# Another order of loads, weight preparation and attention at the start of a fused attention and feed-forward kernel

## The chip, the core and the metric

One core of a Trainium2 chip runs the whole program. Its engines work side by side, each through its own list of instructions in order: TensorE (PE in the profile; its weight loads are PEld), VectorE (DVE), ScalarE (ACT), GpSimd (POOL), and SyncE (SP), which here only starts DMA transfers. An engine that waits for a semaphore holds back everything behind it in its list. The metric is device microseconds from one execution; three timed runs of the kernel before gave 820.78, 822.68 and 823.08 us, so the median is 822.68 us.

## What is computed

```
kv  = einsum('bhsd,bhse->bhde', k, v)          # 8 batches, 8 heads, 576 tokens, head size 64
out = einsum('bhsd,bhde->bhse', q, kv)
x   = out / sqrt(mean(out*out, -1) + 1e-6) * g_norm     # then 4608 tokens x 512
h   = x @ w_in                                  # 512 x 2048
g   = h * tanh(softplus(h))                     # "mish"
y   = g @ w_out                                 # 2048 x 512
```

All in float32, except that the given w_in and w_out are float64, whose two 32-bit words the kernel puts together itself.

## The kernel before, in words

**Tiles and products.** The 4608 tokens are nine tiles of 512. The kernel first makes `g` for all tiles (attention and the first product), writing it to DRAM, and then the second product. Every large float32 operand is split into a high and a low part of the type fp32r (`split`, lines 129 to 131: a cast on ACT at line 130, a subtraction on DVE at line 131), and a product is three matmuls: high by high, high by low, low by high. From tile 1 on, the first product is made with seven block products instead of eight; tile 0 uses the plain eight ("whole" products, `whole_group`).

**Weight units.** `w_in` is cut into eight units (0 to 7). Each goes through six steps (`weight_in`): LOAD (four DMAs of 256 KB of raw words, SP), SCALE (ACT, line 145: the high words read as floats, multiplied), JOIN (DVE, lines 140 to 142: the low words' bits put in), BLOCKS (the split of the four blocks into the tile `wfb`), DIFF and SUMS (differences of blocks on DVE, lines 208 to 210, and their split; needed by the seven-product form). Steps of half a unit are `part_of`. Raw words lie until JOIN in a tile named either `w64` or `wfb<n>`, the place that a later unit's blocks will take. Before, unit 1 loads to the place of wfb5, 2 to wfb6, 3 to wfb7, 5 to wfb6 and 6 to wfb7, and units 0, 4 and 7 to `w64`; so the load of unit 4 waits for the join of unit 0, 5 for that of 2, 6 for that of 3 and 7 for that of 4.

**Slots.** The work is laid out by hand in numbered slots, one slot for one block product of 12 or 24 matmuls. In slot `t` first come evictions (`then`), then the product, then whatever `at(t, ...)` has put there, in the order in which the calls of `at` were made. Each engine's list keeps this order; nothing is reordered later. Tile 0 has slots 0 to 31; pairs of units are used in slots 0 to 7 (units 0, 1), 8 to 15 (2, 3), 16 to 23 (4, 5) and 24 to 31 (6, 7). In slots 24 and on, a slot uses both units of its pair. Tile 1 starts at slot 32 (`T1_`).

**Attention ahead.** While tile 0's products run, the same slots prepare the x of tile 1. `k_load` (line 269) loads a pair of heads of k and v, four pairs a batch, into tiles `km` and `vm` of three buffers each; `k_product` (line 296) multiplies two pairs; `k_keep` (lines 306, 308 on ACT, 311 on DVE) copies the result. For each half `u` of the heads: "transpose" (line 362, PE), "turned" (line 375, a copy out of PSUM on ACT), "project" (line 391, PE), "square" and "scaled" (lines 406 and 414, ACT). Later "sums" (line 430, PE), "rstd" (lines 439 to 441, ACT: a table load, Ln, Exp, and then the table for mish again), "keep" and "spread" (SP, through DRAM), "normalize" (DVE, line 459). Mish (line 127, ACT) empties the product's PSUM banks of names `a` and `bc`, two of each.

**The beginning.** Ahead of slot 0, tile 0's own x is made, with `filler` matmuls of an identity in between (line 687; one filler is two matmul instructions in the trace).

Of the kernel before, what the change touches and what calls it, by code (L numbers as in the profile page):

```python
# [34 lines left out]
def linear_attention_rms_mish_ffn(  # L35
# [622 lines left out]

    conv = {j: weight_in(j, wf_room({1: 5, 2: 6, 3: 7, 5: 6, 6: 7}[j]) if j % 4 and j < 7 else w64_room) for j in range(NF2)}
    LOAD, SCALE, JOIN, BLOCKS, DIFF, SUMS = range(6)  # L660
# [28 lines left out]
    def part_of(j, step, k):  # L689
        conv[j][step](k)  # L690
# [14 lines left out]
    weights(3, LOAD)  # L705
    for r in (slice(0, D), slice(D, P)):
        nc.gpsimd.dma_start(gcol[r, :], g_norm.rearrange("(p o) -> p o", o=1))
    make_identity(nc, ident)
# [8 lines left out]
    def do0(u, m, *steps):  # L717
        for step in steps:
            units[0][u][step](m)

    filler(8)
    do(0, 0, "transpose", "turned")
    filler(10)
    first_kv(0)
    k_keep(0, 0)
    part_of(0, SCALE, 0)
    do(0, 0, "project")
    do0(0, 0, "square")
    do0(0, 1, "square")
    filler(2)  # L730
    part_of(1, SCALE, 0)
    part_of(0, JOIN, 0)
    part_of(1, JOIN, 0)
    do0(0, 0, "sums")
    do0(0, 1, "sums")
    do0(0, 0, "rstd")
    part_of(0, BLOCKS, 0)
    do0(0, 1, "rstd")
    do(0, 1, "transpose")
    do0(0, 0, "normalize")  # L740
# [14 lines left out]
    def slot1():  # L755
        do(0, 1, "project")
        part_of(1, JOIN, 1)
        do0(1, 0, "square")
        do0(1, 1, "square")
        part_of(0, BLOCKS, 1)  # L760
        part_of(2, SCALE, 0)
        part_of(2, JOIN, 0)
        weights(4, LOAD)
        k_load(1, 0)
        k_load(1, 1)
        rows[1] = att.tile([P, H, TR, D], F32, name="qs")
        rows_load(1, 0, H)

    def slot2():
        do0(1, 0, "sums")  # L770
        do0(1, 1, "sums")
        do0(1, 0, "rstd")
        do0(1, 1, "rstd")
        do0(1, 0, "normalize")
        x_whole(A12)
# [14 lines left out]
    T1_ = start(1)  # L790
    for j, t, t2 in ((3, 5, 7), (4, 8, 10), (5, 9, 11), (6, 13, 15), (7, 16, 18)):
        if j > 3:
            at(t, lambda j=j: weights(j, SCALE))
        at(t, lambda j=j: weights(j, JOIN))
        at(t2, lambda j=j: weights(j, BLOCKS))
    for j, t in zip(range(NF2), (19, 21, 23, 25, T1_ + 6, T1_ + 8, T1_ + 13, T1_ + 15)):
        at(t, lambda j=j: weights(j, DIFF))
        at(t + 1, lambda j=j: weights(j, SUMS))
    at(1, lambda: weights(5, LOAD))
    at(1, lambda: k_load(1, 2))  # L800
    at(4, lambda: weights(6, LOAD))
# [15 lines left out]
    def attention(j):  # L817

        def spread():
# [368 lines left out]
```

## Time and profile before

| | |
|---|---|
| median of three timed runs | 822.68 us (820.78 to 823.08) |
| the profiled execution, its own time | 814.41 us |
| its span, first to last instruction | 812.4 us |
| PE busy | 792.8 us (98%) |
| DVE busy | 588.7 us (72%) |
| ACT busy | 443.0 us (55%) |
| PE idle in 0 to 40 us | 7.3 us |
| PE idle in 40 to 60 us | 4.5 us |

In the profile's rows a time is counted from the start of the span. A row of the timeline holds the start, the length, the engine, the line, the operation, the tiles written and read, the shape, how many instructions were merged, and in brackets how long the engine was idle before it and what ended that. "PEclk" is the TensorE clock granted in a stretch, as a share of full speed. The profiled execution was 8.3 us shorter than the median of the timed runs.

### The profile page before, as it was taken

To read this page: it belongs to the slowest core of one execution; us is meant where nothing else is said; L and a number is where in the kernel's file an instruction comes from. 1 tells how busy PE (TensorE), PEld (TensorE's weight loads), DVE (VectorE), ACT (ScalarE), POOL (GpSimd) and SP (SyncE) were. 2 spreads that over 40 slices of the span, in tenths; PEclk is the share of its full clock that TensorE was granted. 3 is DMA by queue.
4 is the path that set the end of the run, shared out by engine and by line. 5 is a ranking of instruction groups with operands and counts; after the bars stand their busy time and mean duration, and the time that the engine had idled before them with its cause. 6 is when DMAs were issued, how large, how long until landed. Compare 5 with 4: busy or idle time off the path is not lost.

```text
span 812.4 us, 16560 instructions
## 1 busy us (share of the span) xinstructions
PE 792.8 (98%) x6752; PEld 723.6 (89%) x6752; DVE 588.7 (72%) x777; ACT 443.0 (55%) x677; POOL 99.1 (12%) x163
## 2 busy tenths in 40 slices
PE   7879999999999999999999999999999999999997
PEld 6779899999999999899999988888888888888886
DVE  2786774668485776757566788888888888878885
ACT  4758575656565566655556654444444444444442
POOL 1011111231323222131311100000000000000000
PEclk9989999999999999999999999999999999999999
DMA  8886787778797887765478943334444444444421
GB/s 298 234 286 189 228 276 214 259 243 303 256 317 260 279 301 201 266 202 194 163 248 283 404 165 130 130 131 139 146 130 130 130 130 130 131 139 146 146 87 53
DMA packets 102859, 164.46 MB, mean 202 GB/s; under 512 B 9088, under 2 KB 69248, under 8 KB 102784
## 3 DMA queue, kind: packets, MB, share of 16 engines
q1 hardware_dynamic: 89184, 116.42, 46.4%
q0 software_dynamic: 13504, 46.93, 15.3%
q8 instruction: 53, 0.87, 0.4%
q14 instruction: 22, 0.18, 0.1%
q10 hardware_dynamic: 96, 0.07, 0.0%
HBM read 106.89 MB, written 56.49 MB: 201 GB/s over the span
## 4 chain that ended last, share of the span: by engine, by line
PE 76%; DMA 6%; issue 6%; DVE 6%; ACT 4%; SPq 2%; POOL 1%; POOLq 0%; ACTq 0%; DVEq 0%
PE a L614 17%; PE a L964 15%; PE bc L614 13%; PE bc L964 11%; PE a L969 8%; PE bc L969 6%; DMA vm<-in_v_dram 2%; DMA wfb<-wod 2%; PE x L397 1%; PE s L296 1%; DMA qs<-in_q_dram 1%; PE ss L430 1%; ACT wfb L130 1%; PE bc L687 1%; PE ss L296 1%
## 5 line engine op out<-in xcount | busy, mean ns | idle before, releaser
L130 ACT CAST gf<-g 128x1024 fp32r<-128x1024 f32 (+1 forms) x104 | 106.5, 1039 | 98.9 <-DVE g L922 64.7
L131 DVE TENSOR_TENSOR gf<-g,gf 128x1024 fp32r<-128x1024 f32 (+1 forms) x104 | 124.1, 1206 | 43.8 <-ACT gf L130 43.7
L964 PE MATMUL a<-wfb,gf 128*128 128x512 f32 x408 | 143.2, 394 | 0.3 <-ACT ow L526 0.3
L614 PE MATMUL a<-gf,wfb 128*128 128x256 f32 x960 | 129.2, 284 | 4.2 <-ACT gf L130 2.7
L614 PEld LDWEIGHTS a<-gf,wfb 128*128 128x128 f32 x960 | 120.5, 192 | 7.7 <-ACT gf L130 3.0
L969 PE MATMUL a<-wfb,gf 128*128 128x256 f32 x408 | 113.1, 277 | 0.0
L614 PE MATMUL bc<-gf,wfb 128*128 128x256 f32 x840 | 109.3, 285 | 0.4 <-DVE gf L131 0.3
L614 PEld LDWEIGHTS bc<-gf,wfb 128*128 128x128 f32 x840 | 104.1, 192 | 4.7 <-issue 2.4
L964 PE MATMUL bc<-wfb,gf 128*128 128x512 f32 x272 | 95.1, 394 | 0.0
L964 PEld LDWEIGHTS a<-wfb,gf 128*128 128x128 f32 x408 | 76.5, 188 | 18.4 <-ACT ow L526 0.6
L969 PEld LDWEIGHTS a<-wfb,gf 128*128 128x128 f32 x408 | 76.5, 188 | 0.0
L969 PE MATMUL bc<-wfb,gf 128*128 128x256 f32 x272 | 75.3, 277 | 0.0
L635 DVE TENSOR_TENSOR ula<-bc,ula 128x512 f32<-128x512 f32 x32 | 22.0, 687 | 58.4 <-PE bc L614 58.4
L964 PEld LDWEIGHTS bc<-wfb,gf 128*128 128x128 f32 x272 | 51.0, 188 | 11.9
L614 PE MATMUL bc<-gf,wfa 128*128 128x256 f32 x384 | 52.0, 285 | 1.2 <-ACT ulb L127 1.2
L127 ACT ACTIVATE ur<-ur 128x1024 f32<-128x1024 f32 x32 | 33.9, 1059 | 35.2 <-DVE ur L635 35.2
L614 PEld LDWEIGHTS a<-a,wfb 128*128 128x128 f32 x384 | 48.3, 192 | 5.0 <-DVE w L150 2.5
L614 PE MATMUL a<-a,wfb 128*128 128x256 f32 x384 | 51.9, 284 | 0.0
L614 PE MATMUL a<-gf,wfa 128*128 128x256 f32 x384 | 51.6, 284 | 0.3
L614 PEld LDWEIGHTS bc<-gf,wfa 128*128 128x128 f32 x384 | 48.3, 191 | 3.6 <-issue 1.5
L969 PEld LDWEIGHTS bc<-wfb,gf 128*128 128x128 f32 x272 | 51.0, 188 | 0.0
L614 PEld LDWEIGHTS a<-gf,wfa 128*128 128x128 f32 x384 | 48.3, 192 | 1.3 <-ACT ur L539 0.7
(205 smaller groups left out, 1433.4 us busy)
## 6 DMA issues: line engine op xcount, KB each, us to landing
g<-gd SPq DMA_DIRECT2D x18, 2048.0 KB
gd<-ur POOLq DMA_DIRECT2D x36, 512.0 KB, 4.8
gd<-ula POOLq DMA_DIRECT2D x36, 256.0 KB, 4.1
gd<-ulb POOLq DMA_DIRECT2D x36, 256.0 KB, 4.7
w<-in_moe_w_out_dram SPq DMA_DIRECT2D x32, 256.0 KB
km<-in_k_dram SPq DMA_DIRECT2D x28, 288.0 KB
vm<-in_v_dram SPq DMA_DIRECT2D x28, 288.0 KB
wfb<-in_moe_w_in_dram SPq DMA_DIRECT2D x20, 256.0 KB
```

The lines of the kernel that those rows point to most:

```text
L127: nc.scalar.activation(o, i, AF.Mish)
L130: nc.scalar.copy(hi, src)
L131: nc.vector.tensor_sub(lo, src, hi.bitcast(F32))
L296: nc.tensor.matmul(outs[a][half(o, a)], kt[half(o), d], vt[half(o), d], start=(c == 0), stop=(c == 8))
L397: nc.tensor.matmul(st["x"][a][half(o), c], kv[r], st["q"][r, a, c], start=True, stop=True)
L430: nc.tensor.matmul(to if j >= T32 else to.rearrange("p (m n) -> p m n", m=2), sel, of, start=True, stop=True)
L614: nc.tensor.matmul(bank[:, jj], w[:, a, kc, :], xf[:, b, kc, :], start=first and jj == kc == s == 0, stop=(kc == 1 and s == 2), skip_group ...
L635: nc.vector.tensor_add(o, bank, o)
L687: nc.tensor.matmul(b[:, 0:P], ident, ident, start=True, stop=True)
L964: nc.tensor.matmul(bank.rearrange("p s (h n) -> p s h n", h=2), gf[:, 0, c, :], wo_form(c, right).rearrange("p h s n -> p s h n"), start=f ...
L969: nc.tensor.matmul(bank[:, 0], gf[:, 1, c, :], wo_form(c, right)[:, :, 0, :], start=False, stop=c == NF2 - 1, skip_group_check=True)
```

## The change

The change has four parts.

1. **Places of the raw words.** Units 1, 2, 3 load to the places of wfb5, wfb6, wfb7 as before; units 4, 5, 6 to wfb4, wfb5, wfb6; only 0 and 7 to `w64`. The load of unit 4 now waits for the last read of tile 0's q (which lies in wfb4), 5 for the join of 1, 6 for that of 2, 7 for that of 0. The loads of units 4 and 5 are issued earlier, those of 6 and 7 behind batch 1's fourth k, v pair.
2. **The head of the program.** The two small DMAs of `gcol` stand behind the identity and the constants on POOL; fillers go from 8, 10, 2, 4 to 4, 7, 2, 0; unit 1's SCALE stands ahead of "square" on ACT; BLOCKS and "normalize" of the first half change places.
3. **Weight steps in the slots.** BLOCKS of unit 4 move from slot 10 to 9; units 6 and 7 from slots 13/15 and 16/18 to 18/20 and 20/22; DIFF and SUMS of units 0 and 1 from slots 19 to 22 to slots 12 to 15.
4. **Attention of tile 1 in the slots.** Batch 1's k products move from slots 7 and 13 to 10 and 17, and tile 1's steps from "transpose" (11) to "spread" (23) one slot later each.

```diff
-    conv = {j: weight_in(j, wf_room({1: 5, 2: 6, 3: 7, 5: 6, 6: 7}[j]) if j % 4 and j < 7 else w64_room) for j in range(NF2)}
+    conv = {j: weight_in(j, w64_room if j in (0, 7) else wf_room(j if j > 3 else j + 4)) for j in range(NF2)}
...
-    for r in (slice(0, D), slice(D, P)):
-        nc.gpsimd.dma_start(gcol[r, :], g_norm.rearrange("(p o) -> p o", o=1))
     make_identity(nc, ident)
...
-    filler(8)
+    for r in (slice(0, D), slice(D, P)):
+        nc.gpsimd.dma_start(gcol[r, :], g_norm.rearrange("(p o) -> p o", o=1))
+
+    filler(4)
     do(0, 0, "transpose", "turned")
-    filler(10)
+    filler(7)
     first_kv(0)
     k_keep(0, 0)
     part_of(0, SCALE, 0)
+    part_of(1, SCALE, 0)
     do(0, 0, "project")
     do0(0, 0, "square")
     do0(0, 1, "square")
     filler(2)
-    part_of(1, SCALE, 0)
     part_of(0, JOIN, 0)
     part_of(1, JOIN, 0)
     do0(0, 0, "sums")
     do0(0, 1, "sums")
-    do0(0, 0, "rstd")
     part_of(0, BLOCKS, 0)
+    do0(0, 0, "rstd", "normalize")
+    part_of(1, BLOCKS, 0)
+    x_whole(A11)
     do0(0, 1, "rstd")
-    do(0, 1, "transpose")
-    do0(0, 0, "normalize")
-    x_whole(A11)
+    do(0, 1, "transpose", "turned")
     do0(0, 1, "normalize")
-    part_of(1, BLOCKS, 0)
     x_whole(A21)
-    do(0, 1, "turned")
-    filler(4)
+    weights(4, LOAD)
...
-        weights(4, LOAD)
+        weights(5, LOAD)
         k_load(1, 0)
         k_load(1, 1)
...
+        k_load(1, 2)
...
-    for j, t, t2 in ((3, 5, 7), (4, 8, 10), (5, 9, 11), (6, 13, 15), (7, 16, 18)):
+    for j, t, t2 in ((3, 5, 7), (4, 8, 9), (5, 9, 11), (6, 18, 20), (7, 20, 22)):
...
-    for j, t in zip(range(NF2), (19, 21, 23, 25, T1_ + 6, T1_ + 8, T1_ + 13, T1_ + 15)):
+    for j, t in zip(range(NF2), (12, 14, 23, 25, T1_ + 6, T1_ + 8, T1_ + 13, T1_ + 15)):
         at(t, lambda j=j: weights(j, DIFF))
         at(t + 1, lambda j=j: weights(j, SUMS))
-    at(1, lambda: weights(5, LOAD))
-    at(1, lambda: k_load(1, 2))
-    at(4, lambda: weights(6, LOAD))
-    at(8, lambda: weights(7, LOAD))
     for n in range(2):
-        at((7, 13)[n], lambda n=n: k_product(1, n))
-        at((8, 14)[n], lambda n=n: k_keep(1, n))
-    at(7, lambda: k_load(1, 3))
+        at((10, 17)[n], lambda n=n: k_product(1, n))
+        at((11, 18)[n], lambda n=n: k_keep(1, n))
+    at(10, lambda: k_load(1, 3))
+    at(10, lambda: weights(6, LOAD))
+    at(11, lambda: weights(7, LOAD))
...
-            (0, 11, "transpose"), (0, 12, "turned"), (0, 13, "project", "square", "scaled"), (1, 15, "transpose"),
-            (1, 16, "turned"), (1, 18, "project", "square", "scaled"), (1, 20, "sums"),
-            (1, 21, "rstd"), (1, 22, "keep"), (0, 23, "spread0"), (0, 28, "normalize"), (1, 29, "normalize"),
+            (0, 12, "transpose"), (0, 13, "turned"), (0, 14, "project", "square", "scaled"), (1, 16, "transpose"),
+            (1, 17, "turned"), (1, 19, "project", "square", "scaled"), (1, 21, "sums"),
+            (1, 22, "rstd"), (1, 23, "keep"), (0, 24, "spread0"), (0, 28, "normalize"), (1, 29, "normalize"),
```

What this does to the engines' lists is shown at three places. In the rows, L145 is a SCALE, L130 into `wfb` a cast of BLOCKS or (behind `wd`) of SUMS, L140 to L142 a JOIN, L131 into `wfb` the subtraction of BLOCKS or SUMS, L306, L308 and L311 a `k_keep`, L375 "turned", L406 and L414 "square" and "scaled", and L127 a mish or the load of its table.

ACT from unit 4's SCALE (slot 8) to the first projection's "square". Before:

```order
L145 ACTIVATE wfa_616<-w_418 128x1024
L306 COPY kv_125<-s_123 128x64
L308 COPY ky_127<-ss 128x64
L145 ACTIVATE wfa_646<-wfb_434 128x1024
L130 CAST wfb_666<-wfa_616 128x4x256
L130 CAST wfb_682<-wfa_646 128x4x256
L375 COPY fh<-x_685 128x1024
L127 ACTIVATE ula<-a 128x512
L145 ACTIVATE wfa_722<-wfb_508 128x1024
L406 ACTIVATE fa<-x_764 128x1024
```

And in the changed kernel:

```order
L145 ACTIVATE wfa_558<-wfb_307 128x1024
L130 CAST wfb_577<-wfa_558 128x4x256
L145 ACTIVATE wfa_580<-wfb_411 128x1024
L130 CAST wfb_659<-wfa_580 128x4x256
L306 COPY kv_125<-s_123 128x64
L308 COPY ky_127<-ss 128x64
L127 ACTIVATE ula<-a 128x512
L130 CAST wfa_712<-wd 128x2x256
L130 CAST wfb_277<-wd 128x2x256
L375 COPY fh<-x_689 128x1024
L127 ACTIVATE ur<-a 128x2x256
L406 ACTIVATE fa<-x_737 128x1024
```

Unit 4's cast now stands ahead of unit 5's SCALE, and "turned" stands behind `k_keep`, one mish and the two casts of unit 0's SUMS.

DVE at the same place, from unit 5's JOIN. Before:

```order
L140 TENSOR_SCALAR wfa_646<-wfa_646 128x1024
L141 SCALAR_TENSOR_TENSOR wfa_646<-wfb_434,wfa_646 128x1024
L142 SCALAR_TENSOR_TENSOR wfa_646<-wfb_434,wfa_646 128x1024
L131 TENSOR_TENSOR wfb_666<-wfa_616,wfb_666 128x4x256
L131 TENSOR_TENSOR wfb_682<-wfa_646,wfb_682 128x4x256
```

And in the changed kernel, where unit 4's subtraction comes first:

```order
L131 TENSOR_TENSOR wfb_577<-wfa_558,wfb_577 128x4x256
L140 TENSOR_SCALAR wfa_580<-wfa_580 128x1024
L141 SCALAR_TENSOR_TENSOR wfa_580<-wfb_411,wfa_580 128x1024
L142 SCALAR_TENSOR_TENSOR wfa_580<-wfb_411,wfa_580 128x1024
L131 TENSOR_TENSOR wfb_659<-wfa_580,wfb_659 128x4x256
L311 COPY ky_127<-s_123 64x64 x2
L311 COPY kv_125<-ss 64x64 x2
L208 TENSOR_TENSOR wd<-wfa_247 128x512
L209 TENSOR_TENSOR wd<-wfa_247,wd 128x256
L210 TENSOR_TENSOR wd<-wfa_247,wd 128x256
L131 TENSOR_TENSOR wfa_712<-wd,wfa_712 128x2x256
L131 TENSOR_TENSOR wfb_277<-wd,wfb_277 128x2x256
```

The join of unit 5 moved behind the subtraction of unit 4, and `k_keep` and DIFF of unit 0 follow the blocks of unit 5.

ACT from the second projection's "square" on. Before, with unit 7's cast just ahead:

```order
L130 CAST wfb_880<-wfa_845 128x4x256
L406 ACTIVATE fh<-x_883 128x1024
L414 ACTIVATE gf<-x_883,gcol 128x2x2x256
L130 CAST wfa_941<-wd 128x2x256
L130 CAST wfb_286<-wd 128x2x256
L127 ACTIVATE ula<-a 128x512
L439 ACT_TABLE_LOAD
L440 ACTIVATE fl<-ss,eps 128x512
L441 ACTIVATE fl<-fl 128x512
L127 ACT_TABLE_LOAD
```

And in the changed kernel:

```order
L406 ACTIVATE fh<-x_891 128x1024
L414 ACTIVATE gf<-x_891,gcol 128x2x2x256
L130 CAST wfb_932<-wfa_867 128x4x256
L145 ACTIVATE wfa_935<-w_668 128x1024
L127 ACTIVATE ula<-a 128x512
L127 ACTIVATE ur<-a 128x2x256
L130 CAST wfb_973<-wfa_935 128x4x256
L439 ACT_TABLE_LOAD
L440 ACTIVATE fl<-ss,eps 128x512
L441 ACTIVATE fl<-fl 128x512
L127 ACT_TABLE_LOAD
L127 ACTIVATE ulb<-bc 128x512
```

Unit 6's cast, unit 7's SCALE and unit 7's cast moved behind the second projection, and the table loads and "rstd" stand behind unit 7's cast.

More of the change, by code (lines that the diff above doesn't have):

```diff
@@ L771, in slot2 @@
         do0(1, 1, "sums")
-        do0(1, 0, "rstd")
+        do0(1, 0, "rstd", "normalize")
         do0(1, 1, "rstd")
-        do0(1, 0, "normalize")
         x_whole(A12)
@@ L795, in linear_attention_rms_mish_ffn @@
         at(t2, lambda j=j: weights(j, BLOCKS))
-    for j, t in zip(range(NF2), (19, 21, 23, 25, T1_ + 6, T1_ + 8, T1_ + 13, T1_ + 15)):
+    for j, t in zip(range(NF2), (12, 14, 23, 25, T1_ + 6, T1_ + 8, T1_ + 13, T1_ + 15)):
         at(t, lambda j=j: weights(j, DIFF))
         at(t + 1, lambda j=j: weights(j, SUMS))
-    at(1, lambda: weights(5, LOAD))
-    at(1, lambda: k_load(1, 2))
-    at(4, lambda: weights(6, LOAD))
-    at(8, lambda: weights(7, LOAD))
     for n in range(2):
-        at((7, 13)[n], lambda n=n: k_product(1, n))
-        at((8, 14)[n], lambda n=n: k_keep(1, n))
-    at(7, lambda: k_load(1, 3))
+        at((10, 17)[n], lambda n=n: k_product(1, n))
[3 more added lines that the diff above has]
+    at(11, lambda: weights(7, LOAD))
     for b in range(2, B):
         t = start(b - 2)
-        loads, made = ((21, 22, 23, 28), (27, T1_ + 2)) if b == 2 else ((0, 3, 10, 11), (9, 17)) if b == 3 else (
+        loads, made = ((22, 23, 24, 28), (27, T1_ + 2)) if b == 2 else ((0, 3, 10, 11), (9, 17)) if b == 3 else (
             (18 - NS, 19 - NS, 1, 2) if b == 4 else (11 - NS, 12 - NS, 1, 2), (0, 10))
```

## The prediction, made before the change was run

> **What bounds the kernel now.** The page comes first: its span and its first row.
>
> ```profile
> span 812.4 us, 16560 instructions
> PE 792.8 (98%) x6752; PEld 723.6 (89%) x6752; DVE 588.7 (72%) x777; ACT 443.0 (55%) x677; POOL 99.1 (12%) x163
> ```
>
> PE is idle for 19.6 us in all, so only that idle time and PE time at a low clock can be won. The view of busy time by stretch shows where they lie (columns: stretch, length, busy time and instructions of PE, PEld, DVE, ACT, POOL, then PEclk, DMA share, GB/s).
>
> ```profile
> 20.30:39.88 19.58, 17.32 (x188) 14.48 (x188) 15.44 (x28) 14.51 (x25) 0.00 (x0) 1.00 0.82 234
> 39.88:51.11 11.23, 11.23 (x157) 10.89 (x156) 9.05 (x13) 6.16 (x10) 2.05 (x3) 1.00 1.07 332
> 51.11:55.58 4.47, 0.00 (x1) 0.03 (x1) 4.40 (x5) 1.62 (x2) 0.00 (x0) 0.78 1.05 372
> 55.58:60.46 4.88, 4.88 (x104) 4.23 (x105) 3.61 (x4) 2.52 (x4) 0.72 (x1) 0.50 0.37 121
> 60.46:77.86 17.40, 17.40 (x167) 15.89 (x167) 10.99 (x18) 14.01 (x20) 2.00 (x3) 1.00 0.60 186
> 93.56:280.00 186.44, 185.90 (x2140) 175.29 (x2140) 121.51 (x191) 111.95 (x187) 46.48 (x72) 1.00 0.80 262
> ```
>
> One hole of 4.47 us stands out, followed by 4.88 us at half clock, which cost another 2.44 us. But DVE was busy for 4.40 of those 4.47 us: it was not waiting. The view of waits names what PE waited for, and the timeline of ACT shows what else was late.
>
> ```profile
> PE ss L296 <- DMA vm<-in_v_dram: 4.5, 1, 4.5
> 53.96 1.04 ACT L130 CAST wfb<-wfa 128x1024 fp32r<-128x1024 f32 x1 [3.17 <-DVE wfa L142]
> 54.91 1.00 ACT L375 COPY fh<-x 128x1024 f32<-128x1024 f32 x1
> 59.80 1.03 ACT L406 ACTIVATE fa<-x 128x1024 f32<-128x1024 f32 x1 [2.36 <-PE x L391]
> ```
>
> PE's wait is for batch 1's fourth v. The copy "turned", without which the first projection can't start, began only at 54.91, behind unit 5's cast, which waited 3.17 us for a join. So two things were late at once: the DMA until 55.58, the preparation of weights until 55.91. Taking the first away leaves the second.
>
> **The change part by part.** *Loads.* With places of their own, units 4 and 5 and the fourth pair come earlier. In the trace the DMA share is 1.05 during the hole: the data were queued behind units 5 and 6, whose loads had waited on joins. In the change the pair follows the k product of slot 10 and leads unit 6, and its own product comes at slot 17, seven slots later: over 10 us for 0.6 MB at the 372 GB/s of the row above, some 2 us. That wait goes. The new waits on SP are for tile 0's q, long read by then, and for unit 1's join, whose last row is
>
> ```profile
> 28.29 0.69 DVE L142 SCALAR_TENSOR_TENSOR wfa<-wfb,wfa 128x512 uint32<-128x512 uint32 x1
> ```
>
> Behind that wait stand batch 1's loads, first needed in slot 10; it ends near 27 with the head's gain, when the queue still holds unit 4. Units 6 and 7 land later but are scaled only in slots 18 and 20.
>
> *The head.* These rows are of the timelines of POOL, PE, SP and ACT.
>
> ```profile
> 1.30 1.21 POOL L707 DMA_DIRECT2D gcol<-in_g_norm_dram  x2 [0.84 <-POOLq L1172]
> 3.13 3.78 PE L687 MATMUL bc<-ident 128*128 128x128 f32 x16 [3.13 <-POOL ident masks.py:199]
> 9.48 1.29 SPq L172 DMA_DIRECT2D w<-in_moe_w_in_dram  x2
> 11.14 0.27 PE L296 MATMUL s<-wfb,wfb 64*64 64x64 f32 x2
> 12.20 0.23 PE L296 MATMUL ss<-wfb,wfb 64*64 64x64 f32 x2
> 12.48 1.50 SPq L172 DMA_DIRECT2D wfb<-in_moe_w_in_dram  x1
> 14.42 0.60 ACT L402 ACTIVATE fa<-x 128x512 f32<-128x512 f32 x1 [1.07 <-PE x L391]
> 15.39 0.67 ACT L145 ACTIVATE wfa<-wfb 128x512 f32<-128x512 f32 x1
> 20.30 0.38 PE L614 MATMUL a<-gf,wfb 128*128 128x256 f32 x1 [1.42 <-ACT gf L130]
> ```
>
> POOL's 1.21 us leave the path to the identity, so PE starts near 1.9; fewer fillers let the first k product start when its v has landed (SP's issue at 9.48 had waited for it), at 9.5 to 9.9 instead of 11.14: 1.5 us. Then unit 1's SCALE, now ahead of the squares on ACT, waits for its words (SP's issue at 12.48 had waited for them) and ends near 13.2; the squares start there, 1.2 us early instead of 1.5. Behind them unit 1's join no longer delays "normalize", worth about another microsecond. I take the first product at 18.1: **2.2 us won**. Bounds: 1.25, if the clock stays at half through the k product (it would then take twice the 1.06 us from 11.14 to 12.20); 2.6, set by the words at 12.48. From there to slot 7 every engine's order is as before, so the gain passes through whole.
>
> *The preparation chain.* These are DVE's rows of units 3 and 5, the copies of `k_keep` and unit 0's DIFF.
>
> ```profile
> 40.15 0.69 DVE L140 TENSOR_SCALAR wfa<-wfa 128x1024 uint32<-128x1024 uint32 x1
> 42.12 1.22 DVE L142 SCALAR_TENSOR_TENSOR wfa<-wfb,wfa 128x1024 uint32<-128x1024 uint32 x1
> 44.47 1.23 DVE L131 TENSOR_TENSOR wfb<-wfa,wfb 128x1024 fp32r<-128x1024 f32 x1 [1.12 <-ACT wfb L130]
> 45.30 1.16 ACT L145 ACTIVATE wfa<-w 128x1024 f32<-128x1024 f32 x1
> 49.74 0.46 DVE L311 COPY ky<-s 64x64 f32<-64x64 f32 x2
> 52.70 1.23 DVE L142 SCALAR_TENSOR_TENSOR wfa<-wfb,wfa 128x1024 uint32<-128x1024 uint32 x1
> 71.05 0.68 DVE L208 TENSOR_TENSOR wd<-wfa 128x512 f32<-128x512 f32 x1
> 72.22 0.42 DVE L210 TENSOR_TENSOR wd<-wfa,wd 128x256 f32<-128x256 f32 x1
> ```
>
> A JOIN takes 3.2 us (40.15 to 43.34), its cast 1.05 on ACT, its subtraction 1.23, a DIFF 1.6 (71.05 to 72.64). Before, from unit 3's join to the end of unit 5's it took 13.8 us (40.15 to 53.93). In the change this stretch loses the copies (0.95), gains unit 4's subtraction (1.23) and 1.1 us in which DVE waits for unit 4's cast: 15.1 us. With the 2.2 us won, unit 3's join starts at 37.95 and unit 5's ends at 53.1. Then unit 5's cast to 54.15, its subtraction to 55.4, the copies to 56.35, DIFF to 57.95, and on ACT the two casts of SUMS, 0.6 each overlapped to 1.1, all of which now stand ahead of "turned": it starts at 59.1 and ends at **60.1**, against 55.91 before.
>
> PE meanwhile has no DMA to wait for. Before, slot 7 ended at 39.88; at 2.2 us less it is 37.7. Slots 8 to 14 at 1.44 us each, a k product of 1.2 and a transpose of 0.8 (rows below, from each start to the next) end at 49.8. So PE stands for **10 us** before the projection in slot 14. Before, the projection began at 57.4, with as much PE work behind it (one slot less, one k product more, row at 57.35): the change is 2.7 us late here. Half clock follows again: by the row of 4.88 us it costs 2.4 us after 60.1, against 1.55 that were left of it before after 57.35: 0.9 more.
>
> [...]
>
> *Units 6 and 7.* Rows of PE from slot 7's k product to the first products of tile 1, and of ACT at "rstd".
>
> ```profile
> 39.88 0.27 PE L296 MATMUL s<-vm,km 64*64 64x64 f32 x2
> 41.09 3.14 PE L614 MATMUL a<-gf,wfb 128*128 128x256 f32 x24
> 46.95 1.03 PE L362 MATMUL x<-ident,qs 128*128 128x128 f32 x8
> 57.35 0.31 PE L391 MATMUL x<-fh,kv 64*64 64x32 f32 x2
> 69.38 0.98 PE L614 MATMUL bc<-gf,wfb 128*128 128x256 f32 x6
> 72.44 0.62 PE L430 MATMUL ss<-fa,sel 128*32 128x512 f32 x2
> 74.33 1.28 ACT L439 ACT_TABLE_LOAD   x1
> 78.29 0.60 ACT L127 ACTIVATE ur<-a 128x512 f32<-128x512 f32 x1
> 90.77 1.60 PE L614 MATMUL a<-gf,wfb 128*128 128x256 f32 x12
> 93.56 1.80 PE L614 MATMUL bc<-gf,wfa 128*128 128x256 f32 x12 [1.19 <-ACT ulb L127]
> ```
>
> Let p be the end of the second projection (slot 19; before it ended at 69.4, a slot earlier in the order). From p, ACT has "square" and "scaled" to p+2.0, unit 6's cast to p+3.0, unit 7's SCALE to p+4.15; DVE its JOIN to p+7.4; then cast to p+8.5 and subtraction to p+9.75. PE reaches unit 7 in the middle of slot 24 after four slots, "sums" (1.0) and half a slot: p+7.5. It waits 1.0 us for the cast and, two matmuls later, 1.0 for the subtraction: **2.0 us**. Behind unit 7's cast come the table loads and "rstd", 3.96 us (74.33 to 78.29), and only then the mish that frees slot 26's bank, done at p+13.05, when slot 25 ended at p+11.7: **1.35 us**. The second projection itself waits some **0.5 us** for its `k_keep`, which stands behind unit 6's join. Before, PE had none of these stalls (17.40 of 17.40 us busy from 60.46): its first is the 1.19 us at 93.56.
>
> *The sum.* The late first projection, 2.7; half clock, 0.9; second projection, 0.5; slots 24 and 26, 3.35; the slot against the k product, -0.2: 7.2 us at tile 1's first product, at 98.0 instead of 90.77. There the old wait of 1.19 us for the x of tile 1 shrinks: DVE's SUMS of units 2 and 3 come some 5.5 late, PE 7.2 late, so up to 1.2 comes back. That is 6.0; with the spread of the head's gain I write **5.8 us**. Behind 93.56 PE is busy 185.90 of 186.44 us and nothing is changed in order, so the loss stays to the end: 814.41 + 5.8 = 820.2 in the profiled execution's terms. The median of the runs is 8.27 us above that execution; I carry that over: 822.68 + 5.8 = **828.5 us**.
>
> **The rivals.** A measurement of this kernel tells about 0.3% from no change: 820.2 to 825.15 counts as the same.
>
> *The v was what mattered* (faster). If "turned" were copied by the time PE gets there, hole, half clock and head are all won: 4.47 + 2.44 + 2.2 = 9.1, so 813.6. The wait list speaks for it, naming only the DMA; the ACT row at 54.91 and DVE's 4.40 us against it: 9 us would have to vanish from a chain of timed instructions. Chance 0.05.
>
> *The timed runs wait longer for the v than the profiled one* (faster or level). They are 8.27 us longer, for a reason that the trace doesn't show. If all of it lay in that one wait, the change would win it back: 828.5 - 8.3 = 820.2. It decides for faster beyond that; slower k, v loads at the start would do it. Against it: such a cause would hardly sit in one place. Chance 0.11.
>
> *Only the first projection is late* (the same). If units 6 and 7 are ready in time, 2.7 + 0.9 + 0.5 - 0.2 = 3.9 remain, of which tile 1's wait takes 1.2: 2.7 to 825.4; with a head gain of 2.6 and a short half clock, 1.3: 824. Chance 0.18.
>
> *A second fall of the clock* (slower still). Slots 24 and 26 together leave 3.35 us idle within about 5; the row of the hole shows that 4.47 are enough. Another 2.4 us, less what later waits take up: 831. Chance 0.1.
>
> The forecast itself, 826 to 830.5, has 0.56.
>
> **How the numbers follow.** Slower by over 0.3%: 0.56 + 0.1 = 0.66. The same: 0.18 of the third rival. Faster: 0.05 + 0.11 = 0.16. The range reaches from 819, which leaves out the first rival and part of the second, to 832, beyond the fourth; the likeliest case's own is 826 to 830.5.
>
> **What would show it.** In the changed profile: no wait of PE on `vm`; the first product near 18.1; "turned" (L375) near 59 behind two casts from `wd`; a PE hole of about 10 us ahead of L391 and half clock behind it; a wait on the cast of `wfb` in the middle of slot 24; tile 1's first product near 98. It would be wrong if "turned" came by 52, which needs unit 5's join to end five microseconds sooner, or if PE's hole ended before 57.

## The result and the profile after

The changed kernel is slower: 830.49 us (median of 21 runs, 823.80 to 835.02) against 820.78 us for the kernel before (21 runs, 814.01 to 823.08). The ratio is 1.0127, with a 95% interval of 1.0099 to 1.0156: some 10 us lost where 5.8 were forecast. The profiled execution of the change took 835.02 us, with a span of 833.0 us. It is the longest of the 21, so not every wait and low clock that its trace shows need stand in the others.

The page's first row, which answers the one that opened the prediction (PE was busy for 792.8 us of 812.4):

```profile
span 833.0 us, 16514 instructions
PE 803.2 (96%) x6730; PEld 729.3 (88%) x6730; DVE 589.0 (71%) x777; ACT 443.9 (53%) x677; POOL 99.1 (12%) x163
```

PE's idle time went from 19.6 to 29.8 us. Its waits in the first 140 us of the changed kernel (engine, line, what ended the wait; total, times, longest):

```profile
PE x L391 <- ACT fh L375: 10.1, 1, 10.1
PE bc L614 <- ACT ulb L127: 2.7, 1, 2.7
...
PE a L614 <- DVE wfb L131: 0.8, 1, 0.8
PE a L614 <- ACT wfb L130: 0.7, 1, 0.7
```

The wait for `vm` is gone. In its place PE waits 10.1 us for "turned". ACT's timeline of the changed kernel shows why:

```profile
54.58 1.04 ACT L130 CAST wfb<-wfa 128x1024 fp32r<-128x1024 f32 x1 [3.72 <-DVE wfa L142]
...
55.73 0.61 ACT L127 ACTIVATE ula<-a 128x512 f32<-128x512 f32 x1
59.57 0.62 ACT L130 CAST wfa<-wd 128x512 fp32r<-128x512 f32 x1 [3.22 <-DVE wd L210]
60.09 0.61 ACT L130 CAST wfb<-wd 128x512 fp32r<-128x512 f32 x1
60.61 1.00 ACT L375 COPY fh<-x 128x1024 f32<-128x1024 f32 x1
...
85.92 0.63 ACT L441 ACTIVATE fl<-fl 128x512 f32<-128x512 f32 x1
```

The same step in the kernel before:

```profile
76.35 0.63 ACT L441 ACTIVATE fl<-fl 128x512 f32<-128x512 f32 x1
```

ACT itself is idle for 3.22 us, because the next thing in its list is the cast of SUMS, which needs DIFF from DVE; "turned", which needs nothing any more, stands behind it. The last row of the timeline is the end of "rstd" of tile 1 (Exp). It was at 76.35 before, 14.4 us ahead of the first product of tile 1 at 90.77; now it is at 85.92, 12.9 us ahead of it at 98.82. What hangs on it shows in DVE's rows of "normalize" and in PE's row of tile 1's second product:

```profile
96.39 1.23 DVE L459 TENSOR_TENSOR gf<-gf,fh 128x1024 f32<-128x1024 f32 x1 [1.98 <-DMA fh<-rd]
...
100.18 1.23 DVE L459 TENSOR_TENSOR gf<-gf,fa 128x1024 f32<-128x1024 f32 x1 [1.18 <-DMA fa<-rd]
```

```profile
103.33 1.88 PE L614 MATMUL bc<-gf,wfa 128*128 128x256 f32 x7 [2.72 <-ACT ulb L127]
```

The row names a mish (`ulb`). ACT's rows just ahead of it show what that mish stood behind:

```profile
102.16 0.62 ACT L130 CAST gf<-s 128x512 fp32r<-128x512 f32 x1 [2.91 <-DVE s L478]
102.69 0.59 ACT L127 ACTIVATE ulb<-bc 128x512 f32<-128x512 f32 x1
```

And the second "normalize" of the kernel before, which did not wait for the DMA:

```profile
90.41 1.22 DVE L459 TENSOR_TENSOR gf<-gf,fa 128x1024 f32<-128x1024 f32 x1
```

"normalize" waits for "spread", the round trip of rstd through DRAM; the cast of the x that is made from it waits for "normalize", and the mish that PE waits for stands behind that cast. That product started at 93.56 before, after a wait of 1.19 us; I call its start **the mark** below, since nothing behind it is changed in order. It is 9.8 us late in this execution, and the second product starts 14.3 us late (491.65 against 477.31): the low clock behind the mark adds 2, and some 2.5 us more arise further behind, which was not followed. The stretches at a low clock, in the view of busy time by stretch (the eighth group of columns is PEclk):

```profile
17.19:20.60 3.41, 1.81 (x12) 1.56 (x12) 2.59 (x4) 2.91 (x7) 0.00 (x0) 1.00 1.10 348
...
20.60:24.01 3.41, 3.41 (x79) 3.20 (x78) 1.44 (x5) 1.60 (x6) 0.00 (x0) 0.50 1.10 348
...
61.67:64.97 3.30, 3.30 (x37) 2.40 (x38) 1.42 (x3) 1.45 (x3) 0.00 (x0) 0.50 0.00 0
...
85.45:88.87 3.42, 3.42 (x17) 3.41 (x17) 1.15 (x3) 3.36 (x6) 0.00 (x0) 0.50 0.02 7
...
102.52:109.35 6.83, 6.02 (x88) 5.68 (x89) 5.15 (x8) 3.97 (x9) 1.29 (x2) 0.50 0.39 133
```

The kernel before had one such stretch here, behind its hole. The changed one has four: in the head (20.60), behind the hole (61.67), in slots 24 and 25 (85.45), and at the mark (102.52). The first row is the stretch ahead of the first of them.

One thing has to be known before times are compared. The second product of the kernel (`y`) takes 330.6 us in some of the profiled executions and 336.8 in others; the last section shows it. The times of one kernel lie in two groups some 6 us apart to match. In the runs above, 6 of 21 of the kernel before (to 817.17) and 10 of 21 of the change (to 828.35) lie in the lower group. Group against group the means differ by 11.1 and 12.0 us, so the 9.7 us between the medians understate the loss. Ratios below are over 12 runs (21 for the change, 6 for the first experiment) against the kernel before on the same chip, whose median was 819 to 821 us on some chips and 814 on others; the mark, which lies ahead of all that, stands beside them. Two executions with a mean granted clock far below the rest (0.753 in 959.14 us of the kernel before, 0.656 in 1091.07 us of the one with unit 4's blocks behind "turned"; 0.986 to 1.000 in the others) are left out of the ratios.

### The profile page after: what moved, and what is told of

It is laid out like the page before. It is cut to its first block, busy times and chain, and to the rows that moved or that the text cites. A ratio compares the mean times of both kernels' runs of the same rounds, so it can differ in the third digit from the quotient of the medians.

```text
span 833.0 us, 16514 instructions
## 1 busy us (share of the span) xinstructions
PE 803.2 (96%) x6730; PEld 729.3 (88%) x6730; DVE 589.0 (71%) x777; ACT 443.9 (53%) x677; POOL 99.1 (12%) x163
## 4 chain that ended last, share of the span: by engine, by line
PE 77%; DMA 6%; DVE 5%; issue 5%; ACT 3%; SPq 2%; POOL 1%; ACTq 0%; POOLq 0%; DVEq 0%
PE a L614 18%; PE a L960 15%; PE bc L614 13%; PE bc L960 11%; PE a L965 8%; PE bc L965 6%; DMA fa<-rd 2%; PE s L296 2%; DMA wfb<-wod 2%; PE x L397 1%; PE ss L430 1%; ACT wfb L130 1%; DVE wfa L141 1%; DMA gd<-ulb 1%; DVE gf L131 1%
## 5 line engine op out<-in xcount | busy, mean ns | idle before, releaser
L130 ACT CAST gf<-g 128x1024 fp32r<-128x1024 f32 (+1 forms) x104 | 106.4, 1038 | 94.8 <-DVE g L918 64.7
L131 DVE TENSOR_TENSOR gf<-g,gf 128x1024 fp32r<-128x1024 f32 (+1 forms) x104 | 124.1, 1206 | 43.7 <-ACT gf L130 43.7
L960 PE MATMUL a<-wfb,gf 128*128 128x512 f32 x408 | 145.9, 399 | 0.3 <-ACT ow L526 0.3
L614 PE MATMUL a<-gf,wfb 128*128 128x256 f32 x960 | 132.2, 287 | 6.4 <-ACT gf L130 2.3
L614 PEld LDWEIGHTS a<-gf,wfb 128*128 128x128 f32 x960 | 122.5, 194 | 10.4 <-ACT gf L130 2.7
L960 PE MATMUL bc<-wfb,gf 128*128 128x512 f32 x272 | 96.9, 399 | 0.0
L960 PEld LDWEIGHTS a<-wfb,gf 128*128 128x128 f32 x408 | 76.7, 188 | 19.6 <-ACT ow L526 0.6
L127 ACT ACTIVATE ur<-ur 128x1024 f32<-128x1024 f32 x32 | 33.9, 1059 | 35.2 <-DVE ur L635 35.2
```

The source lines that it names most:

```text
L127: nc.scalar.activation(o, i, AF.Mish)
L130: nc.scalar.copy(hi, src)
L131: nc.vector.tensor_sub(lo, src, hi.bitcast(F32))
L614: nc.tensor.matmul(bank[:, jj], w[:, a, kc, :], xf[:, b, kc, :], start=first and jj == kc == s == 0, stop=(kc == 1 and s == 2), skip_group ...
L960: nc.tensor.matmul(bank.rearrange("p s (h n) -> p s h n", h=2), gf[:, 0, c, :], wo_form(c, right).rearrange("p h s n -> p s h n"), start=f ...
```

## The experiments

| kernel | mark, us | ratio to before, 95% interval |
|---|---|---|
| before | 93.56 | 1 |
| the change (parts 1 to 4) | 103.33 | 1.0127 [1.0099, 1.0156] |
| change, DIFF and SUMS of units 0, 1 two slots later | 99.22 | 1.0098 [1.0060, 1.0137] |
| change, units 6 and 7 back | 98.68 | 1.0049 [1.0014, 1.0083] |
| parts 1, 2, 4 (weight steps back) | 96.67 | 1.0063 [1.0032, 1.0093] |
| parts 1, 2, 3 (attention back) | 94.56 | 0.9996 [0.9965, 1.0027] |
| part 1 alone (loads) | 93.24 | 0.9977 [0.9946, 1.0008] |
| part 2 alone (head) | 91.24 | 0.9970 [0.9939, 1.0001] |
| parts 1, 2 (loads and head) | 89.43 | 0.9948 [0.9917, 0.9979] |
| loads and head, sums to spread one slot later | 91.71 | 0.9983 [0.9948, 1.0018] |
| loads and head, unit 5's blocks behind "turned" | 88.64 | 0.9939 [0.9910, 0.9969] |
| the same, unit 4's too | 88.57 | 0.9957 [0.9922, 0.9991] |
| loads and head, unit 5's behind, k product at 9 | 92.04 | 0.9976 [0.9945, 1.0006] |
| the same, four fillers kept | 89.79 | 0.9981 [0.9942, 1.0020] |

**DIFF and SUMS of units 0 and 1 later.** The changed kernel with

```diff
-    for j, t in zip(range(NF2), (12, 14, 23, 25, ...
+    for j, t in zip(range(NF2), (14, 16, 23, 25, ...
```

> The changed kernel with DIFF of units 0 and 1 at slots 14 and 16 instead of 12 and 14 (SUMS at 15 and 17), nothing else. Theory (weight preparation ahead of "turned" makes the hole): "turned" of the first half no longer stands behind DIFF and two casts of SUMS and starts near 57 instead of 60.61; PE's hole ahead of the first projection shrinks from 10.1 us to about 6.5; the two stalls of slots 24 and 26 stay; the time is 3 to 4 us below the changed kernel's, near 826.5. Rival (the head, or attention one slot later as such, loses the time): "turned" may come earlier, but the start of tile 1's second product (103.33) and the time stay within 1 us.

PE's waits from 0 to 140 us of this kernel:

```profile
PE x L391 <- ACT fh L375: 5.0, 1, 5.0
...
PE bc L614 <- ACT ulb L127: 3.0, 2, 1.9
...
PE x L391 <- DVE ky L311: 1.7, 1, 1.7
...
PE a L614 <- DVE wfb L131: 0.8, 1, 0.8
```

The hole halves, from 10.1 to 5.0 us, so the casts of SUMS made the other 5.1. Only 4.1 of them arrive at the mark, and 2.4 us in the time (0.0029 of 820 us, the intervals overlapping): a new wait of 1.7 us stands at the second projection, whose `k_keep` copies on DVE come behind unit 6's join. The join waited 1.20 us for its SCALE, which stands on ACT behind the later casts of SUMS and the second "turned". And the waits behind units 6 and 7 are all still there.

**Units 6 and 7 back.** The changed kernel with

```diff
-    ... (5, 9, 11), (6, 18, 20), (7, 20, 22)):
+    ... (5, 9, 11), (6, 13, 15), (7, 16, 18)):
```

> The changed kernel with units 6 and 7 back at slots 13/15 and 16/18, nothing else (DIFF and SUMS of units 0 and 1 stay at 12 to 15). Theory: "turned" stays near 60.6 or later (SCALE of unit 6 is ahead of it now too: up to 1 us), PE's hole stays 10 us; the stalls on unit 7 in slots 24 go, of those at slot 26 and before tile 1's second product as much as in the run with the old table stays (1.4 and 2.5); second product of tile 1 near 101, 3 us before the changed kernel's. Rival (the stalls of slots 24 and 26 are only the late first projection passed on): no gain.

```profile
PE x L391 <- ACT fh L375: 10.1, 1, 10.1
...
PE x L391 <- DVE ky L311: 0.8, 1, 0.8
...
PE bc L614 <- ACT ulb L127: 0.2, 1, 0.2
```

These are its waits of PE. The hole is as long as in the change, the waits of slot 24 are gone, and so is the wait ahead of the mark, which I had expected to stay at 1.4 and 2.5 us. The mark comes 4.65 us earlier, though the first projection does not. So the late units did not just pass the hole on: with unit 7's cast ahead of the table loads they made "rstd" late, and through "spread" the x of tile 1. ACT's rows agree: Exp starts 5.6 us behind the second "square" here (82.72 and 77.08) and 10.5 us behind it in the change (85.92 and 75.47).

**Weight steps back, attention later (parts 1, 2, 4).** The changed kernel with

```diff
-    ... (4, 8, 9), (5, 9, 11), (6, 18, 20), (7, 20, 22)):
+    ... (4, 8, 10), (5, 9, 11), (6, 13, 15), (7, 16, 18)):
-    for j, t in zip(range(NF2), (12, 14, 23, 25, ...
+    for j, t in zip(range(NF2), (19, 21, 23, 25, ...
```

> The changed kernel with the weight steps of the kernel before (part 3 undone: BLOCKS of unit 4 at 10, units 6 and 7 at 13/15 and 16/18, DIFF and SUMS of units 0 and 1 at 19 to 22); loads, head and attention one slot later stay. Theory: "turned" stands behind unit 5's cast and unit 6's SCALE alone and ends near 56; the stalls of slots 24 and 26 and the late rstd go; no second, third or fourth fall of the clock; tile 1's second product starts at or before 93.6, time 817 to 821. Rival (loads, head or the later attention lose the time): it stays at 826 to 831.

Its waits of PE from 50 to 110 us, and DVE's rows of "normalize":

```profile
PE x L391 <- ACT fh L375: 4.7, 1, 4.7
PE bc L614 <- ACT ulb L127: 3.9, 2, 2.5
PE a L614 <- ACT ula L127: 0.5, 1, 0.5
```

```profile
89.91 1.22 DVE L459 TENSOR_TENSOR gf<-gf,fh 128x1024 f32<-128x1024 f32 x1 [2.48 <-DMA fh<-rd]
...
93.52 1.23 DVE L459 TENSOR_TENSOR gf<-gf,fa 128x1024 f32<-128x1024 f32 x1 [1.00 <-DMA fa<-rd]
```

My theory, that part 3 alone loses the time, falls. "turned" did end at 55.9 as expected, but the mark is at 96.67, not at 93.6, and the time is 0.63% above the kernel before. Attention one slot later costs by itself: one step of it, "turned", by standing behind unit 6's SCALE too, which waited 0.99 us for its words, and another, "rstd", by standing behind one more pair of casts, so that "spread" is waited for.

**Attention back (parts 1, 2, 3).** Loads and head (the kernel with parts 1 and 2, further below) with part 3's numbers:

```diff
-    ... (4, 8, 10), (5, 9, 11), (6, 13, 15), (7, 16, 18)):
+    ... (4, 8, 9), (5, 9, 11), (6, 18, 20), (7, 20, 22)):
-    for j, t in zip(range(NF2), (19, 21, 23, 25, ...
+    for j, t in zip(range(NF2), (12, 14, 23, 25, ...
```

> The changed kernel with part 4 undone (attention steps and k products in the slots of the kernel before), part 3 kept. "turned" now stands in slot 12, ahead of the casts of SUMS though behind DIFF's slot. If the 10 us hole comes from part 3 and part 4 together (SUMS ahead of "turned" only because both moved), "turned" runs at 53 as with loads and head alone, the hole is near 3 us, the stalls on units 6 and 7 stay (3 to 5 us), tile 1's second product starts at 92 to 96, time 817 to 822. If part 3 alone makes the hole, it stays at 8 us or more and the time at 826 or more.

```profile
PE x L391 <- ACT fh L375: 5.2, 1, 5.2
...
PE a L614 <- ACT wfb L130: 1.0, 1, 1.0
PE a L614 <- DVE wfb L131: 0.8, 1, 0.8
```

As expected for an effect of both parts: with "turned" in slot 12 again, it stands ahead of the casts of SUMS, and the hole is 5.2 us (3 expected: unit 4's blocks at slot 9 put its cast and subtraction ahead of unit 5's join). The mark lies in the forecast band, and the time is that of the kernel before, as the band had it against some 820 us.

**Part 1 alone, part 2 alone, and both.** The loads: the kernel before with the places of the raw words and the early LOADs of the change, and the fourth pair, still in slot 7, ahead of units 6 and 7:

```diff
+    conv = {j: weight_in(j, w64_room if j in (0, 7) else wf_room(j if j > 3 else j + 4)) for j in range(NF2)}
...
     at(7, lambda: k_load(1, 3))
+    at(7, lambda: weights(6, LOAD))
+    at(8, lambda: weights(7, LOAD))
```

> The kernel before with part 1 alone: places of the raw words as in the change, loads of units 4 and 5 and batch 1's third pair early, the fourth pair ahead of units 6 and 7; all steps in the slots as before. Theory: PE's wait for vm of 4.5 us goes, but the projection then waits for "turned", which still stands behind unit 5's cast and ends near 55.9: a hole of about 3.6 us, the clock falls or not; 1 to 1.5 us gained, 819 to 820 against 820.8. Rival (the v was what mattered): hole and half clock both go, 6.9 us gained, 814.

The head: the kernel before with the second part of the change, from `gcol` to the last filler:

```diff
-    filler(8)
+    filler(4)
     do(0, 0, "transpose", "turned")
-    filler(10)
+    filler(7)
...
+    part_of(1, SCALE, 0)
     do(0, 0, "project")
...
-    filler(4)
```

> The kernel before with part 2 alone (fillers 4, 7, 2, 0; gcol behind the constants; SCALE of unit 1 ahead of the squares; BLOCKS and normalize in the new order). Prediction: 2.2 us earlier at the first product, all kept, so v is waited for 2 us longer and nothing is won before the hole ends at 55.58, where the DMA rules: 0 to -1 us in time. Reading of the changed kernel: the first product 1.9 us earlier, a fall of the clock between 20 and 24 us, 0.7 to 1.2 us of it lost. Rival (the head causes the loss of 10 us): 3 us or more slower than before.

Both together, the steps in the slots of the kernel before:

> The kernel before with parts 1 and 2 (loads and head) and neither part 3 nor part 4. Its distance to the run with the old weight table (start of tile 1's second product at 96.67) is the price of part 4. Theory: the head's 2.2 us and the early loads bring slot 12 to 49, but "turned" still stands behind unit 5's cast and ends near 53: a hole of 2 to 3 us, tile 1's second product at 90 to 91, time 816 to 817.5. Rival (the two parts only win where each alone wins, about 2 us each of noise): no better than 818.

The waits of PE from 30 to 110 us with loads and head:

```profile
PE x L391 <- ACT fh L375: 3.3, 1, 3.3
...
PE bc L614 <- ACT ulb L127: 0.4, 1, 0.4
PE ss L296 <- DMA vm<-in_v_dram: 0.4, 1, 0.4
```

With the loads alone, PE's wait of 4.5 us for v became one of 2.8 us for "turned" and one of 0.8 for a v at slot 7: little is won, and the rival that v was what mattered, with 6.9 us to win, falls. The head alone is a gain or nothing. That the DMA would hold PE there until 55.58 was wrong: PE went on at 53.27, and the mark came 2.3 us earlier. Neither is the culprit, and together they make a kernel that is faster than the one before: 0.9948, 4.1 us earlier at the mark.

Part 4 is here the moved steps with the moved k products and the loads behind them. Two moves of the change that its diff above leaves out count with it too: batch 2's first k, v pairs go from slots 21, 22, 23 to 22, 23, 24, and in slot 2 one "normalize" of tile 0 goes ahead of the second "rstd". With four of these kernels the price of parts 3 and 4 can be read twice (ratios, and the mark):

| added to loads and head | ratio | mark |
|---|---|---|
| nothing | 0.9948 | 89.43 |
| part 3 | 0.9996 | 94.56 |
| part 4 | 1.0063 | 96.67 |
| both | 1.0127 | 103.33 |

Part 3 costs 0.48% alone and 0.64% on top of part 4; part 4 costs 1.15% and 1.31%. They nearly add, and the later attention is the larger, some 9 to 11 us of 820 against 4 to 5. Each ratio carries 0.3%, so a difference of two carries some 0.4%: part 3's 0.48% is hardly clear of that, part 4's price is.

The traces of loads and head and of parts 1, 2, 4 show where the 7.2 us of part 4 at the mark arise. The product of slot 24 starts at 77.09 instead of 74.49, 2.6 us late, and 0.9 of that was there at the end of slot 7 (38.78 against 37.84), behind a low clock in the head (0.50 from 32.5 to 35.9 us), which part 4 does not change. A wait of 1.41 us for the mish behind the table loads of "rstd" and one of 0.51 for the mish behind the first "normalize" then bring tile 1's first product to 92.33 instead of 87.40, 4.9 us late, and the wait of 2.52 us at the mark, against 0.43, makes the 7.2. So some 2.6 us come through "spread" and 1.4 through the table loads, in one execution each.

**Only the second half of part 4.** Loads and head with

```diff
-            ... (1, 20, "sums"), (1, 21, "rstd"), (1, 22, "keep"), (0, 23, "spread0"), ...
+            ... (1, 21, "sums"), (1, 22, "rstd"), (1, 23, "keep"), (0, 24, "spread0"), ...
```

> Loads and head (the run that was faster than the kernel before) with only the second half of part 4: sums, rstd, keep and spread of tile 1 in slots 21 to 24 instead of 20 to 23; "turned", the projections and the k products stay. Theory: rstd's Exp ends some 4 to 5 us later (behind two more casts and a mish), the spread through DRAM that was hidden (no wait of normalize) is then waited for by 2 to 3 us, and the mish of slot 26 stands behind the table loads: PE waits 1 to 1.4 us in slot 26 and 2 to 2.5 us at tile 1's second product, which starts at 92 to 93.5 instead of 89.43; time 818 to 819.5 against 815.2 with loads and head. Rival (the price of part 4 is the late "turned" alone, and the spread only follows it): second product at 89.5 to 90.5, 815 to 816.

```profile
88.56 1.23 DVE L459 TENSOR_TENSOR gf<-gf,fa 128x1024 f32<-128x1024 f32 x1 [1.06 <-DMA fa<-rd]
```

Exp of "rstd" ended at 76.93 instead of 72.86, the 4 us expected, but of the spread's cover only 1.06 us was missing. PE's waits in slot 26 and at the mark are 0.4 and 1.1 us against 0 and 0.4: 1.1 us more, where 3 were expected. The rest of the 2.3 us at the mark I put down to the clock: behind the hole it was at half for 6.8 us here (53.18 to 60.00), for 3.4 with loads and head (55.26 to 58.67). So the mechanism is there, and by itself it explains one of the seven microseconds of part 4.

But this kernel leaves out one thing that parts 1, 2, 4 have, the later k, v pairs of batch 2. SP's rows from the write of rstd on, first here, then with parts 1, 2, 4:

```profile
76.96 1.19 SPq L445 DMA_DIRECT2D rd<-fl  x4
78.61 1.28 SPq L452 DMA_DIRECT2D fh<-rd  x2
```

```profile
79.60 1.19 SPq L445 DMA_DIRECT2D rd<-fl  x4
80.89 0.36 SPq L269 DMA_DIRECT2D km<-in_k_dram  x1
81.31 0.42 SPq L269 DMA_DIRECT2D vm<-in_v_dram  x1
81.91 1.68 SPq L452 DMA_DIRECT2D fh<-rd  x2
```

Here no pair stands between write and read, and the second "normalize" starts 11.6 us behind the end of Exp; there it starts 14.0 us behind it (93.52 and 79.57). So this kernel understates what the late "rstd" costs in the change. How the remaining six microseconds divide between the late "turned", the clock, these loads and the spread is not separated by an experiment.

**"turned" first.** Three attempts to take the remaining 3.3 us. With unit 5's blocks at slot 13, behind "turned":

```diff
-    ... (5, 9, 11), (6, 13, 15), ...
+    ... (5, 9, 13), (6, 13, 15), ...
```

> Loads and head (the run that was faster than the kernel before) with the blocks of unit 5 at slot 13 instead of 11, so that "turned" no longer stands behind unit 5's cast; the k products stay at 7 and 13. Theory: "turned" runs at 49 to 50, behind unit 4's cast, and PE's wait of 3.3 us ahead of the projection and the half clock behind it go: 3 to 4 us; unit 6's and 7's chains gain only 1 us, so up to 1.5 of it is lost again at the second projection or at tile 1's second product, which starts at 85.5 to 87.5 (loads and head: 89.43); time 811 to 813.5. Rival: all of it is lost again to the chain behind, second product at 89 or later, 815.

```profile
PE ss L296 <- DMA vm<-in_v_dram: 2.3, 1, 2.3
PE bc L614 <- ACT ulb L127: 1.4, 1, 1.4
```

The wait for "turned" is gone. In its place PE waits 2.3 us for a v at slot 7, so that "turned" itself waited for PE, and 1.4 us at the mark. With 0.9939 it is the fastest of the study and beats both kernels, though it can't be told from loads and head alone, and it won 0.8 us at the mark where 2 to 4 were forecast. With unit 4's blocks behind "turned" as well:

```diff
-    ... (4, 8, 10), (5, 9, 13), ...
+    ... (4, 8, 13), (5, 9, 13), ...
```

> As the run with unit 5's blocks at slot 13, with unit 4's blocks at 13 too (from 10): "turned" runs ahead of both casts, at 46 to 47. Theory: 0.3 us more at most than with unit 5's alone, since PE reaches the projection at 50.7 anyway; what unit 4's and 5's later subtractions do to unit 6's join costs 0 to 1 us. Time 811 to 814. Rival: unit 4's blocks are late for slot 16, 816 or more.

And with unit 5's blocks at 13 and the first k product two slots later, the loads behind it too (tried ahead of these two, on loads and head):

```diff
-        at((7, 13)[n], lambda n=n: k_product(1, n))
-        at((8, 14)[n], lambda n=n: k_keep(1, n))
-    at(7, lambda: k_load(1, 3))
-    at(7, lambda: weights(6, LOAD))
-    at(8, lambda: weights(7, LOAD))
+        at((9, 13)[n], lambda n=n: k_product(1, n))
+        at((10, 14)[n], lambda n=n: k_keep(1, n))
+    at(9, lambda: k_load(1, 3))
+    at(9, lambda: weights(6, LOAD))
+    at(10, lambda: weights(7, LOAD))
```

> The run before (loads and head) with the blocks of unit 5 moved from slot 11 to 13, so that "turned" stands ahead of unit 5's cast on ACT, and the first k product moved from slot 7 to 9 with the fourth pair's load behind it. Theory: "turned" ends near 49, before PE gets there, no hole at 50 to 56 and no fall of the clock behind it; tile 1's second product at 84.5 to 87; time 811 to 813.5. Rival: the wait moves on (unit 5's or unit 6's blocks late by as much, or the spread), second product at 90 or later, 816 or more.

With both units' blocks behind "turned" PE had no wait between the head and slot 15, and still came to the same mark, 88.57: it waited 1.1 us for "scaled", 0.9 for a mish, 1.4 at the mark. With the k product at slot 9, PE's wait moved to the second k product:

```profile
53.69 0.48 PE L296 MATMUL s<-vm,km 64*64 64x64 f32 x4 [3.33 <-ACT wfb L130]
```

```profile
53.13 0.46 DVE L311 COPY ky<-s 64x64 f32<-64x64 f32 x2
53.61 0.46 DVE L311 COPY kv<-ss 64x64 f32<-64x64 f32 x2
```

Here the view names a cast, but what the product needed was the banks `s` and `ss` of the first k product, which the copies of `k_keep` empty. These copies stood behind unit 5's join and unit 4's subtraction, and the first ended at 53.59, when PE went on. In the two kernels that reach the mark at 88.6, "normalize" starts without a wait right behind DVE's SUMS, 0.1 us apart (82.98 and 82.90), though PE had waited at different places. So with PE fast enough the chain of DVE and ACT seems to decide; no kernel with a shorter chain was run.

**Four fillers kept.** The last kernel (k product at 9) with the fillers ahead of slot 0 again:

```diff
+    filler(4)
     weights(4, LOAD)
```

> The run before with the four fillers ahead of slot 0 kept (eight matmuls, some 1 us of PE, in time in which PE waits for normalize). If the idle time at 17 to 18 us that their removal leaves is what lowers the clock between 20 and 33 us, the stretch from the first product to slot 7 is 1 to 1.7 us shorter; if the fall comes from the idle stretches between the first products themselves, it is the same to 0.3 us, or later by what the fillers hold up.

It reached the end of slot 7 at 37.5 and had no low clock there (1.00 from 12 to 39 us), but loads and head had none either (1.00 from 12 to 39 us), without the fillers. From the first product to slot 8 it took 19.55 us (18.06 to 37.61), as without them (19.66 to 39.21); there, too, the clock was 1.00 in that stretch. That the fillers guard the clock is neither shown nor refuted; the time is the same within its interval.

## Why the prediction was right, and where it was not

*The v wait goes, "turned" becomes the wait.* Right, by its own rows: "turned" at 60.61 where 59.1 was worked out, a hole of 10.1 us where 10 was, though both its ends came 1.6 to 1.8 us later than worked out.

*The head, 2.2 us, "so the gain passes through whole".* The first product came at 18.45 (18.1 forecast, 1.85 us early), but slot 8 only 0.85 us early when the k product that left slot 7 is set aside (39.03, against 41.09 less 1.2). The row at 20.60 is what took it: half clock for 3.41 us, behind a stretch in which PE had been busy for 1.81 of 3.41 us. Loads and head and two of its variants, which have the same head and had no low clock there, ended slot 7 at 37.4 to 37.8, 2.0 to 2.5 us early, so the term was right for them. The step left out that this head came with 3.41 us at half clock in one execution and with none in another.

*The first projection, half clock, units 6 and 7.* 7.2 us were summed up to tile 1's first product; it came at 98.82 instead of 90.77, 8.05. The difference of 0.85 is a balance. The first projection began at 61.67 instead of 57.35, 4.3 us late where 2.7 were summed; much of that is the part of the head that was lost. Against it, half clock lasted 3.30 us behind the restart, where 4.88 were taken, and so cost 0.1 us more than before instead of 0.9. No run shows the source of the "short half clock" in the third rival's sum: behind the hole of before half clock lasted 4.88 us from the restart, and in the changed kernel 3.30. Slot 24 waited 0.7 for the cast and 0.8 for the subtraction (2.0 forecast). Slot 26 did not wait: slots 24 and 25 ran at half clock instead, and its bank was free by the time. That is the fourth rival, in the place where it was put. The wait of the second projection for `k_keep` (0.5) did not come.

*"There the old wait of 1.19 us for the x of tile 1 shrinks ... so up to 1.2 comes back."* This is the step that failed. The wait grew to 2.72 us, and inside it the clock fell, for 6.83 us: where 6.0 were to be left, the mark was 9.8 us late and the next products 11.8. Nor did the loss only "stay to the end": it was 14.3 us where the second product starts. The step counted only DVE's DIFF and SUMS there, and not "rstd" and its way through DRAM, though the sum itself had put "rstd" behind unit 7's cast. Taking units 6 and 7 back cut that wait to 0.2 us and brought the mark from 103.33 to 98.68.

*Which part costs.* The prediction gave the loss to the weight steps (part 3) and took the later attention as a shift of work. The runs give part 4 the larger share, 1.15 to 1.31% against 0.48 to 0.64%.

*The base.* 8.27 us between the profiled execution and the median were carried over as unknown. They are mostly the two lengths of the second product, 6.2 us apart; that execution had the short one. The second rival, which put those 8 us into the wait for v, falls with the loads alone, which took the wait away and won 0.2%, within its interval. With more runs the median of before is 820.78 instead of 822.68, which hides 2 of the 4 us by which the loss was underestimated: 828.5 was forecast and 830.49 came. That 830.49 lies so near is therefore in part luck: a loss of 9.7 us on the base of the forecast is 832.4, and group against group the loss was 11 to 12 us, twice the 5.8.

## What to carry to other kernels

Where an engine takes its list in order, ask of each moved step not only what it costs but what stands behind it that was ready: here copies of 1 us stood behind casts that waited 3 us for another engine. Follow every value that has a long way (a round trip through DRAM) from its first instruction to its last reader, and check that the cover is still there. Idle time of PE can cost more than it lasts, and not in every execution: inside the wait of 2.72 us at the mark the clock fell, and was at half for 6.83 us, while with loads and head it stayed at 1.00 behind 3.42 us in which PE was busy for only 1.82.

## What the runs showed of the hardware

**The stretches at half clock are multiples of 3.41 us.** In the changed kernel's trace they last 3.41, 10.24, 3.42 and 6.83 us (the second, behind the hole, began inside it, at 54.73); a third of 10.24 is 3.413. They begin on one grid: from 20.60 to 54.73 are 34.13 us, ten times 3.413, to 85.45 are 64.85, 19 times, and from there to 102.52 are 17.07, five times. Ahead of the first stands a stretch, from 17.19 to 20.60, in which PE was busy for 1.81 of 3.41 us, or 53%; of the 3.41 us ahead of the other three it was busy for 0.29, 1.93 and 1.51. Half clock does not always follow: with loads and head, a stretch eight times 3.41 us ahead of its low clock at 55.26 was as empty as the first, and the clock stayed at 1.00 behind it:

```profile
27.95:31.37 3.42, 1.82 (x14) 1.41 (x12) 2.70 (x5) 2.36 (x4) 0.00 (x0) 1.00 0.85 271
```

In the changed kernel PE was busy for 3.41, 3.30, 3.42 and 3.42 us of the last 3.41 or 3.42 at half clock, ahead of each return to 1.00. Where the sums to "spread" were one slot later, PE was busy for 3.08 of 3.42 us from 53.18 on, and the clock stayed at half for 3.4 us more.

**The second product has two speeds.** The view of busy time by stretch, the same 60 us of the second product, in the kernel before and in the one with the loads alone:

```profile
680.00:740.00 60.00, 60.00 (x348) 52.44 (x347) 48.85 (x47) 28.42 (x36) 0.00 (x0) 1.00 0.43 132
```

```profile
680.00:740.00 60.00, 60.00 (x342) 52.05 (x341) 48.08 (x46) 27.92 (x35) 0.00 (x0) 1.00 0.43 133
```

PE is busy without a gap, the clock is 1.00 in both, the data rate is 132 and 133 GB/s, and yet 348 matmuls pass in one and 342 in the other. Their groups in the two traces:

```profile
L964 PE MATMUL bc<-wfb,gf x272: 392/394/395, 486.3 to 802.1; 128*128 128x512 f32 x136
```

```profile
L964 PE MATMUL bc<-wfb,gf x272: 395/398/403, 484.8 to 806.7; 128*128 128x512 f32 x136
```

Of the 14 profiled executions, 5 had the short second product (330.5 to 330.6 us from the start of its first matmul to the start of its last) and 9 the long one (336.8), with nothing in between, and the times of the kernel before fall into two groups to match (814.0 to 817.2 and 819.2 to 823.1). What sets it was not found.
